# Retention and two feed-forward layers: attention by halves of 64 tokens, the first 512-token block through all of d_ff, operands of layer two kept as two halves

## The chip, the cores and the metric

One core of a Trainium2 chip runs the kernel. Its engines work side by side and meet at semaphores: PE (TensorE, matmuls), DVE (VectorE), ACT (ScalarE), POOL (GpSimd) and SP (SyncE, which only issues transfers). The metric is the device time of one execution in microseconds; the median of three runs counts.

## The reference, cut to what matters

Four batches of eight heads, 576 tokens each, head size 64: causal attention without softmax, in which a score decays with the distance. Its result, 2304 tokens of 512 numbers, goes through two feed-forward layers of width 2048. All in float32; the weights come as float64.

```python
scores = scale * np.matmul(q, k.transpose(0, 1, 3, 2))
gamma = 1.0 - 2.0 ** (-5.0 - np.arange(H, dtype=np.float32))
Dmat = np.where(rel >= 0, gamma[:, None, None] ** rel[None, :, :], 0.0)
attn_out = np.matmul(scores * Dmat, v)          # rel[i, j] = i - j
x = attn_out by tokens, heads side by side       # 2304 x 512
h = x @ w_in;  x = np.maximum(0.01 * h, h) @ w_out      # layer one
h = x @ w_in2; out = (h * np.cos(h)) @ w_out2           # layer two
```

## The kernel before

**Feed-forward.** The 2304 tokens lie in five blocks (`TB`, 384 or 512 tokens), d_ff in 16 tiles of 128 (`f`). A step of the program takes one block and one tile: `h_mm` (L327) forms h for it in 12 products, `o_mm` (L344) adds the tile of two steps before (three in layer two) to the block's output in 12 more, four banks of PSUM at a time. Twelve, since a float32 operand is split into a high half and a low rest, and three of the four combinations are formed for each of four pieces of 128: `split` (L232 on ACT, L233 on DVE) does it for x, `g_high` (L391, ACT) and `g_low` (L397, DVE) for g. In layer one g is 0.01 h on ACT (L381) and the larger of that and h on DVE (L382); in layer two the cosine by five DVE and three ACT instructions. `evacuate` copies a finished block out of PSUM and stores it.

**Attention** goes by chunks of 128 tokens and turns of two pairs of heads (`duo`), with a running state per pair. `scores` (L165) forms 128x128 scores and masks them on DVE (L170); `values` reads the state (L183), adds the values (L190, L191), forms the chunk's addition to the state (L196), scales the result on ACT (L205) and adds to the state on DVE (L215, L217). POOL scales q and v of a chunk ahead (L142, L146).

**Weights.** Each half tile (128x512 float64) is read as words (`load_raw`) and turned into float32 by two ACT instructions (`conv_a`: L255, L256) and four on DVE (`conv_b`: L261, L263, L266; `conv_c`: L273), then split by ACT (`conv_d`, L276) and, from the third on, POOL (`conv_e`, L280). Layer two's weights are converted the same way during layer one (`stash`), stored as float32, fetched again during layer one's last block and split there (`split_w`).

**Order.** Attention of the first block (three chunks) comes first, with products that nothing reads between its turns (`warm`, L226). Then six tiles of d_ff for block 0, all 16 for block 1, the other ten for block 0, whose two parts of output are added, and the other blocks; attention for the next block is spread over the steps. Up to step `MANUAL` = 22 the scheduler of the framework sets the order in each engine's queue, from then on that of the program. In either case an engine takes its queue strictly in order.

## Time and profile before

| | us |
|---|---|
| median of three runs | 924.25 (923.59 to 926.24) |
| span of the profiled execution | 923.9 |
| PE busy | 905.6 (98%) |
| DVE busy | 652.4 (71%) |
| ACT busy | 403.4 (44%) |
| POOL busy | 139.1 (15%) |

The profile is of one execution. A matmul's end in it is modelled, and consecutive matmuls overlap, so the pace of TensorE is better read from starts than from durations. The chain of work that ended last runs over PE for 87% of the span and over DVE for 10%.

### The profile page before, as it was taken

To read this page: it belongs to the slowest core of one execution; us is meant where nothing else is said; L and a number is where in the kernel's file an instruction comes from. 1 tells how busy PE (TensorE), PEld (TensorE's weight loads), DVE (VectorE), ACT (ScalarE), POOL (GpSimd) and SP (SyncE) were. 2 spreads that over 40 slices of the span, in tenths; PEclk is the share of its full clock that TensorE was granted. 3 is DMA by queue.
4 is the path that set the end of the run, shared out by engine and by line. 5 is a ranking of instruction groups with operands and counts; after the bars stand their busy time and mean duration, and the time that the engine had idled before them with its cause. 6 is when DMAs were issued, how large, how long until landed. Compare 5 with 4: busy or idle time off the path is not lost.

```text
span 923.9 us, 13238 instructions
## 1 busy us (share of the span) xinstructions
PE 905.6 (98%) x5052; PEld 772.6 (84%) x5052; DVE 652.4 (71%) x1155; ACT 403.4 (44%) x758; POOL 139.1 (15%) x112
## 2 busy tenths in 40 slices
PE   9899988999999999999999999999999999999998
PEld 8676866788987788999888888888889998888998
DVE  4988889556746566665222698788778889878885
ACT  3554655443433354444444643353334344334433
POOL 3555333112210011100144420000000000000000
PEclk9999999999999999999999999999999999999999
DMA  9356533146453445432333240020011001000100
GB/s 346 124 172 208 158 117 133 46 147 220 144 168 108 143 149 179 166 135 81 103 92 103 81 136 0 1 81 1 1 34 58 1 26 44 1 1 1 46 1 35
DMA packets 37951, 87.55 MB, mean 95 GB/s; under 512 B 4480, under 2 KB 9728, under 8 KB 37888
## 3 DMA queue, kind: packets, MB, share of 16 engines
q1 hardware_dynamic: 37312, 86.26, 27.7%
q8 instruction: 39, 0.64, 0.3%
q10 hardware_dynamic: 576, 0.45, 0.1%
q14 instruction: 24, 0.20, 0.1%
HBM read 67.30 MB, written 19.40 MB: 94 GB/s over the span
## 4 chain that ended last, share of the span: by engine, by line
PE 87%; DVE 10%; issue 2%; ACT 1%; DMA 0%; DVEq 0%; ACTq 0%
PE o L344 40%; PE h L327 28%; PE at L327 11%; DVE t L266 3%; PE at L165 2%; DVE t L273 2%; PE at L191 2%; DVE t L263 2%; DVE t L261 2%; PE at L183 2%; PE o L226 1%; PE at L196 1%; ACT t L255 1%; DVE x_sb L233 1%; DMA raw<-in_w 0%
## 5 line engine op out<-in xcount | busy, mean ns | idle before, releaser
L344 PE MATMUL o<-g,w 128*128 128x512 f32 (+1 forms) x1920 | 427.1, 370 | 5.0 <-DVE g L397 3.4
L344 PEld LDWEIGHTS o<-g,w 128*128 128x128 f32 x1920 | 348.7, 188 | 55.3 <-DVE g L397 7.1
L327 PE MATMUL h<-x_sb,w 128*128 128x512 f32 (+1 forms) x1440 | 323.6, 371 | 6.2 <-DVE x_sb L233 3.6
L327 PEld LDWEIGHTS h<-x_sb,w 128*128 128x128 f32 x1440 | 260.3, 188 | 47.3 <-DVE x_sb L233 5.1
L391 ACT CAST g<-graw 128x512 fp32r<-128x512 f32 (+1 forms) x160 | 92.5, 578 | 237.0 <-DVE graw L421 93.6
L397 DVE TENSOR_TENSOR g<-graw,g 128x512 fp32r<-128x512 f32 (+1 forms) x152 | 99.8, 657 | 40.3 <-ACT g L391 40.2
L280 POOL TENSOR_TENSOR w<-t,w 128x512 fp32r<-128x512 f32 x62 | 82.4, 1340 | 181.5 <-ACT w L276 175.8
L327 PE MATMUL at<-x_sb,w 128*128 128x512 f32 (+1 forms) x480 | 105.2, 367 | 0.0
L415 ACT ACTIVATE r_sb<-r_sb 128x512 f32<-128x512 f32 (+1 forms) x80 | 47.3, 591 | 131.8 <-DVE r_sb L414 131.8
L327 PEld LDWEIGHTS at<-x_sb,w 128*128 128x128 f32 x480 | 87.7, 188 | 11.5
L382 DVE TENSOR_TENSOR graw<-graw,h 128x512 f32<-128x512 f32 (+1 forms) x80 | 50.2, 627 | 43.5 <-ACT graw L381 43.5
L170 DVE TENSOR_TENSOR p_sb<-at,mask_sb 128x256 f32<-128x256 f32 x66 | 25.5, 418 | 60.7 <-PE at L165 60.6
L381 ACT ACTIVATE graw<-h 128x512 f32<-128x512 f32 (+1 forms) x80 | 44.2, 553 | 42.2 <-PE h L327 37.1
L266 DVE SCALAR_TENSOR_TENSOR t<-raw,t 128x512 uint32<-128x512 uint32 x64 | 57.9, 905 | 1.8
L255 ACT ACTIVATE t<-raw 128x512 f32<-128x512 f32 x64 | 42.9, 670 | 29.9 <-DMA raw<-in_w 27.5
L413 DVE SCALAR_TENSOR_TENSOR r_sb<-t_sb,r_sb 128x512 f32<-128x512 f32 (+1 forms) x80 | 52.1, 652 | 2.8
L414 DVE SCALAR_TENSOR_TENSOR r_sb<-t_sb,r_sb 128x512 f32<-128x512 f32 (+1 forms) x80 | 51.1, 639 | 2.7
L142 POOL TENSOR_TENSOR q_sb<-q_sb,itab_sb 128x512 f32<-128x512 f32 x18 | 25.9, 1441 | 169.3 <-DMA q_sb<-in_qt 165.5
L276 ACT CAST w<-t 128x512 fp32r<-128x512 f32 x64 | 39.0, 618 | 27.9 <-DVE t L273 26.8
L273 DVE CUSTOM_DVE_ANT_0 t<-raw,t 128x1024 uint16<-128x1024 uint16 x64 | 48.7, 762 | 2.4
L416 ACT ACTIVATE r_sb<-r_sb 128x512 f32<-128x512 f32 (+1 forms) x80 | 47.2, 589 | 2.5
L256 ACT ACTIVATE raw<-raw 128x512 int32<-128x512 uint32 x64 | 42.6, 666 | 1.8 <-DMA raw<-in_w 1.8
(52 smaller groups left out, 607.2 us busy)
## 6 DMA issues: line engine op xcount, KB each, us to landing
raw<-in_w SPq DMA_DIRECT2D x64, 512.0 KB, 3.4
kv_sb<-in_kv SPq DMA_DIRECT2D x16, 512.0 KB, 5.6
w<-t SPq DMA_DIRECT2D x32, 256.0 KB, 2.2
t<-w SPq DMA_DIRECT2D x32, 256.0 KB, 2.7
q_sb<-in_qt SPq DMA_DIRECT2D x18, 256.0 KB, 3.7
kt_sb<-in_kt SPq DMA_DIRECT2D x18, 256.0 KB, 4.1
x<-o_sb SPq DMA_DIRECT2D x12, 256.0 KB, 7.1
xr<-x SPq DMA_DIRECT2D x12, 256.0 KB, 4.5
```

The lines of the kernel that those rows point to most:

```text
L255: nc.scalar.activation(t, hi.bitcast(F32), AF.Abs)
L266: nc.vector.scalar_tensor_tensor(out=u, in0=words[:, :, 1], scalar=0xC0000000, in1=u, op0=ALU.bitwise_and, op1=ALU.bitwise_or)
L273: eng.tensor_tensor(out=i, in0=i, in1=lo, op=ALU.add)
L280: eng.tensor_tensor(out=wt[:, 1, s], in0=t_t.pop((l, f, s)), in1=wt[:, 0, s].bitcast(F32), op=ALU.subtract)
L327: nc.tensor.matmul(hp[:, :n], wt[:, i, 0, ks], x_t[lj, k][:, j, :n], start=(k == 0 and a == 0), stop=(k == KK - 1 and a == 2),)
L344: nc.tensor.matmul(o_t[lj, m][:, :n], wt[:, i, 1, ms], gt[:, j, :n], start=(f in starts and a == 0), stop=(f + 1 in ends and a == 2),)
L382: nc.vector.tensor_tensor(out=g, in0=g, in1=hp, op=ALU.max)
L391: nc.scalar.copy(g_t[lj, f][:, 0, : TB[lj % NB]], g)
L397: eng.tensor_tensor(out=gt[:, 1, :n], in0=graw.pop((lj, f)), in1=gt[:, 0, :n].bitcast(F32), op=ALU.subtract)
L413: nc.vector.scalar_tensor_tensor(out=r, in0=t, scalar=-C2, in1=r, op0=ALU.mult, op1=ALU.add)
L414: nc.vector.scalar_tensor_tensor(out=r, in0=t, scalar=-C3, in1=r, op0=ALU.mult, op1=ALU.add)
L415: nc.scalar.activation(r, r, AF.Sin, scale=0.5)
```

## The change

- **Attention by halves.** A chunk is still 128 tokens, but products are between halves of 64: scores only within a half, the state after each half (`state`, now four pairs wide, two additions of 128x256 a chunk instead of four of 128x64). Every product is 64x64x64 on a quarter of the array. All four head pairs go together; `scores`, `values` and the new `reads` are placed at three places of a step. q, k and v of a chunk come in one transfer of 1 MB.
- **Order.** Blocks are 512, 512, 512, 384, 384 tokens and each goes through all of d_ff at once, block 0 as well. The start does four chunks; the other 14 come at every third or fourth step. From step 0 on the order is that of the program.
- **Weights.** 15 of the 16 tiles of layer one are read and converted whole (1 MB, instructions of 128x1024), the last in two halves. The conversion keeps to four tiles in the start and then one a step; its last subtraction is on DVE.
- **Layer two's operands** are stored as the two halves that the products use: `stash_w` splits a converted half tile (ACT, POOL) and stores 512 KB, `fetch_w` reads them straight into place; `evacuate` of layer one splits x (ACT, DVE) and stores both halves, `load_x` reads both.
- **Prelu** on ACT replaces the product with 0.01 and the maximum. PSUM is one tile, its banks named by number. `G`, the buffers for what comes out of a product, is 4 instead of 5.

```diff
-TB = (384, 512, 512, 384, 512)
-T0 = (0, 384, 896, 1408, 1792)
+
+TB = (512, 512, 512, 384, 384)
+T0 = (0, 512, 1024, 1536, 1920)
...
-MANUAL = 22
...
-WARM = (28, 2, 6)
...
-G = 5
+WHOLE = NF - 1
...
+MANUAL = 0
...
+WARM = (16, 2)
...
+G = 4
...
+    psum = psp.tile([P, 8, 512], F32, name="psum")
...
+    def scores(i):
+        b, ch = banks_of(i), ch_t[i]
+        for p in range(NP):
+            for x in range(2):
+                for e, r in enumerate(halves):
+                    t = slice(p * P + x * C, p * P + (x + 1) * C)
+                    nc.tensor.matmul(
+                        psum[halves[x], b + e, p * C : (p + 1) * C],
+                        ch[r, 1, t],
+                        ch[r, 0, t],
+                        start=True,
+                        stop=True,
...
+            out=pt,
+            in0=psum[:, b : b + 2, : NP * C].rearrange("p e (n c) -> p e n c", n=NP),
+            in1=mask_sb.unsqueeze(1).unsqueeze(1).to_broadcast([P, 2, NP, C]),
+            op=ALU.mult,
...
+    def values(i):
+        b, ch, pt = banks_of(i), ch_t[i], p_t.pop(i)
+        local = [(2 * i + x) % SUBS for x in range(2)]
+        for p in range(NP):
+            for x, tok in enumerate(halves):
+                for e, r in enumerate(halves):
+                    h = slice((2 * p + e) * D, (2 * p + e + 1) * D)
+                    o = NP * C + p * C
+                    nc.tensor.matmul(
+                        psum[r, b + x, o : o + C],
+                        ch[tok, 3, h],
+                        pt[tok, e, p, :],
+                        start=p == 0,
+                        stop=local[x] == 0,
+                        skip_group_check=True,
...
+                        psum[r, b + x, p * D : (p + 1) * D],
+                        ch[tok, 2, h],
+                        ch[tok, 3, h],
...
+            new = ap.tile([P, NP * D], F32, tag="st", name="st", bufs=3)
+            add = psum[:, b + x, : NP * D]
+            if local[x] == 0:
+                summed[i] = nc.vector.tensor_copy(new, add)
+            else:
+                summed[i] = nc.vector.tensor_tensor(out=new, in0=add, in1=state[2 * i + x], op=ALU.add)
...
+    def reads(i):
...
+                    read = nc.tensor.matmul(
+                        psum[r, b + x, o : o + C],
+                        st[r, p * D : (p + 1) * D],
+                        ch[r, 0, t : t + C],
...
+    def load_raw(f):
+        if f < WHOLE:
...
+            raw = wp.tile([P, 2 * DM], I64, tag=f"w{tag}", name="raw")
+            nc.sync.dma_start(raw, w[0, f])
...
+    def stash_w(g):
+        t = t_t.pop(g)
+        both = rawp_t[g].rearrange("p (a n) -> p a n", a=2).bitcast(F32R)
+        nc.scalar.copy(both[:, 1], t)
+        nc.gpsimd.tensor_tensor(
+            out=both[:, 0], in0=t, in1=both[:, 1].bitcast(F32), op=ALU.subtract
+        )
+        nc.sync.dma_start(w2[g[1]][g[2]], rawp_t.pop(g).rearrange("p (a n) -> p a n", a=2))
+
+
+    def fetch_w(f):
+        new_w(1, f)
+        for s in range(2):
+            nc.sync.dma_start(w_t[1, f][:, :, s * DM : (s + 1) * DM].bitcast(F32), w2[f][s])
...
+            hi = gp.tile([P, n], F32R, tag="graw", name="x_hi", bufs=G)
...
+            nc.scalar.copy(hi, src)
+            nc.vector.tensor_tensor(out=lo, in0=src, in1=hi.bitcast(F32), op=ALU.subtract)
+            nc.sync.dma_start(x2[j][m][:, 0], hi.bitcast(F32))
+            nc.sync.dma_start(x2[j][m][:, 1], lo.bitcast(F32))
...
-        nc.scalar.mul(g, hp, 0.01)
-        nc.vector.tensor_tensor(out=g, in0=g, in1=hp, op=ALU.max)
+        nc.scalar.activation(g, hp, AF.Prelu, alpha=0.01)
...
+    grains = [(0, f, None) for f in range(WHOLE)]
+    grains += [(0, f, s) for f in range(WHOLE, NF) for s in range(2)]
...
-                    conv_e(*grains[k - 1], nc.vector if k < 3 else nc.gpsimd)
...
+                    conv_e(g, nc.vector)
...
-    turns = [(0, 0, PART), (1, 0, NF), (0, PART, NF)] + [(j, 0, NF) for j in range(2, NB)]
-    turns += [(NB + j, 0, NF) for j in (*range(1, NB), 0)]
...
+    turns = [*range(NB), *range(NB, 2 * NB)]
...
+            chunk_at[s1 + 2 + x * (NF - 4) // len(chunks[j + 1])] = i
...
+        warm(WARM[0], 3)
+        scores(0)
+        for i in range(n_first):
+            if i + 1 < n_first:
+                scores(i + 1)
+            warm(WARM[1], banks_of(i) ^ 4)
+            values(i)
+            conv(1)
+            warm(WARM[1], banks_of(i) ^ 4)
+            reads(i)
...
+                if s < NF:
+                    want = 2 * min(len(grains), max(n_first, s + 4)) + 1
+                    conv(min(1, want - halves_done[0]))
                 h_mm(lj, f)
...
+                leaky(lj, f)
+                if s < NF:
+                    conv(max(0, want - halves_done[0]))
+                g_high(lj, f)
+            for q in outs.get(s, ()):
+                o_mm(*q)
+            if i is not None:
+                reads(i)
+                if i + 2 < NCH:
+                    load_chunk(i + 2)
+                    ahead(i + 2)
+            if s + 1 in chunk_at:
+                scores(chunk_at[s + 1])
```

What it does to the rows of an engine is seen at three places.

PE in layer one, a place where attention stands between the groups of the feed-forward (`at` is the attention's bank, h and o the feed-forward's). Before, one turn of two head pairs:

```order
L165 MATMUL at<-q_sb,kt_sb 128x128 x4
L327 MATMUL h<-x_sb,w_774 128x384 x12
L183 MATMUL at<-q_sb,state_123 64x128 x2
L183 MATMUL at<-q_sb,state_124 64x128 x2
L191 MATMUL at<-p_sb,kv_sb 64x128 x4
L196 MATMUL at<-kv_sb 64x64 x4
L344 MATMUL o_1141<-g,w_1446 128x512 x3
```

Now (all banks are in `psum`; L160 are scores, L184 values, L198 the addition to the state, L227 reads of the state, L379 h and L393 o), one chunk:

```order
L160 MATMUL psum<-ch 64x64 x16
L379 MATMUL psum<-x_sb,w_679 128x512 x12
L184 MATMUL psum<-p_sb,ch 64x64 x16
L198 MATMUL psum<-ch 64x64 x16
L393 MATMUL psum<-g,w_567 128x512 x12
L227 MATMUL psum<-ch,st 64x64 x16
L379 MATMUL psum<-x_sb,w_744 128x512 x12
```

The reads of the state have moved behind the o group, the products are smaller and four times as many in a row.

DVE while layer one's weights are converted (t is a tile in conversion). Before, in block 1:

```order
L397 TENSOR_TENSOR g<-graw,g 128x512
L273 ISA t_1006<-raw,t_1006 128x1024
L382 TENSOR_TENSOR graw<-graw,h 128x512
L261 TENSOR_SCALAR t_1048<-t_1048 128x512
L263 TENSOR_SCALAR t_1048<-t_1048 128x512
L266 SCALAR_TENSOR_TENSOR t_1048<-raw,t_1048 128x512
L397 TENSOR_TENSOR g<-graw,g 128x512
L273 ISA t_1048<-raw,t_1048 128x1024
```

Now, in block 0, a step with a chunk (L300 to L312 convert, L324 is the last subtraction, L169 the mask, L214 the state, L439 the low half of g):

```order
L324 TENSOR_TENSOR w_785<-t_741,w_785 128x1024
L169 TENSOR_TENSOR p_sb<-psum,mask_sb 128x512
L300 TENSOR_SCALAR t_782<-t_782 128x1024
L302 TENSOR_SCALAR t_782<-t_782 128x1024
L305 SCALAR_TENSOR_TENSOR t_782<-raw,t_782 128x1024
L312 ISA t_782<-raw,t_782 128x2048
L214 TENSOR_TENSOR st<-psum,st 128x256 x2
L439 TENSOR_TENSOR g<-graw,g 128x512
L324 TENSOR_TENSOR w_880<-t_782,w_880 128x1024
```

The maximum is gone, the subtraction has come from POOL, the instructions are twice as wide, and the mask of the next chunk stands behind a whole conversion.

DVE at the end of the start, where x of the first block is split (L366). Now:

```order
L300 TENSOR_SCALAR t_514<-t_514 128x1024
L302 TENSOR_SCALAR t_514<-t_514 128x1024
L324 TENSOR_TENSOR w_517<-t_440,w_517 128x1024
L305 SCALAR_TENSOR_TENSOR t_514<-raw,t_514 128x1024
L366 TENSOR_TENSOR x_sb<-xr,x_sb 128x512
L312 ISA t_514<-raw,t_514 128x2048
L366 TENSOR_TENSOR x_sb<-xr,x_sb 128x512 x3
```

Before, the first block's x (L233) stood among the conversion of half tiles:

```order
L261 TENSOR_SCALAR t_420<-t_420 128x512
L233 TENSOR_TENSOR x_sb<-xr,x_sb 128x384
L263 TENSOR_SCALAR t_420<-t_420 128x512
L233 TENSOR_TENSOR x_sb<-xr,x_sb 128x384
L266 SCALAR_TENSOR_TENSOR t_420<-raw,t_420 128x512
L233 TENSOR_TENSOR x_sb<-xr,x_sb 128x384
```

Ahead of its last piece stand now four whole tiles in conversion, where there were five half tiles.

## Rows read from the trace of the kernel before

**Rows 1.** Stages: us, busy us (count) of PE, PEld, DVE, ACT, POOL; clock; DMA; GB/s.

```profile
31.20:86.60 55.40, 51.00 (x386) 37.92 (x385) 47.02 (x88) 28.57 (x64) 26.06 (x20) 0.97 0.47 158
86.60:184.50 97.90, 89.49 (x386) 70.80 (x385) 77.83 (x111) 54.17 (x98) 30.11 (x22) 1.00 0.36 124
184.50:911.50 727.00, 727.00 (x3961) 631.12 (x3961) 505.34 (x907) 302.20 (x560) 69.99 (x56) 1.00 0.24 78
911.50:923.90 12.40, 8.64 (x50) 8.19 (x48) 4.54 (x9) 4.31 (x9) 0.00 (x0) 0.99 0.18 64
```

**Rows 2.** PE in order of time, feed-forward alone; start, us, engine, line, operation.

```profile
448.77 2.88 PE L327 MATMUL h<-x_sb,w 128*128 128x512 f32 x12
...
454.21 2.88 PE L327 MATMUL h<-x_sb,w 128*128 128x512 f32 x12
...
715.88 2.24 PE L344 MATMUL o<-g,w 128*128 128x384 f32 x12
...
720.04 2.24 PE L344 MATMUL o<-g,w 128*128 128x384 f32 x12
```

**Rows 3.** PE in order of time, one turn of attention between two groups.

```profile
191.81 0.71 PE L165 MATMUL at<-q_sb,kt_sb 64*128 64x128 f32 x8
192.45 2.38 PE L327 MATMUL h<-x_sb,w 128*128 128x384 f32 x12
194.76 0.65 PE L183 MATMUL at<-q_sb,state 64*64 64x128 f32 x8
195.35 0.66 PE L191 MATMUL at<-p_sb,kv_sb 128*64 128x128 f32 x8
195.83 0.40 PE L196 MATMUL at<-kv_sb 128*64 128x64 f32 x8
196.16 3.02 PE L344 MATMUL o<-g,w 128*128 128x512 f32 x12
```

**Rows 4.** PE in order of time, values of a chunk that two sequences share.

```profile
53.07 0.27 PE L191 MATMUL at<-p_sb,kv_sb 128*64 128x64 f32 x1
53.08 0.27 PE L190 MATMUL at<-p_sb,kv_sb 128*64 128x64 f32 x1
...
53.24 0.22 PE L191 MATMUL at<-p_sb,kv_sb 128*64 128x64 f32 x1
...
53.30 0.27 PE L191 MATMUL at<-p_sb,kv_sb 128*64 128x64 f32 x2
```

**Rows 5.** DVE in order of time, block 1 during the conversion.

```profile
131.36 0.69 DVE L266 SCALAR_TENSOR_TENSOR t<-raw,t 128x512 uint32<-128x512 uint32 x1
131.97 0.69 DVE L397 TENSOR_TENSOR g<-graw,g 128x512 fp32r<-128x512 f32 x1
132.57 0.69 DVE L273 CUSTOM_DVE_ANT_0 t<-raw,t 128x1024 uint16<-128x1024 uint16 x1
133.17 0.68 DVE L382 TENSOR_TENSOR graw<-graw,h 128x512 f32<-128x512 f32 x1
133.77 0.42 DVE L261 TENSOR_SCALAR t<-t 128x512 f32<-128x512 f32 x1
134.22 1.40 DVE L263 TENSOR_SCALAR t<-t 128x512 uint32<-128x512 uint32 x1
```

**Rows 6.** ACT in order of time, the same place.

```profile
131.96 0.67 ACT L255 ACTIVATE t<-raw 128x512 f32<-128x512 f32 x1 [0.63 <-DMA raw<-in_w]
132.53 0.69 ACT L256 ACTIVATE raw<-raw 128x512 int32<-128x512 uint32 x1
133.29 0.62 ACT L276 CAST w<-t 128x512 fp32r<-128x512 f32 x1
```

**Rows 7.** POOL in order of time, the same place.

```profile
133.99 1.35 POOL L280 TENSOR_TENSOR w<-t,w 128x512 fp32r<-128x512 f32 x1 [3.41 <-ACT w L276]
```

**Rows 8.** Transfers at the start: a stretch, with GB/s last; raw tiles, median to landing.

```profile
5.00:10.00 5.00, 5.00 (x46) 4.88 (x46) 0.00 (x0) 0.00 (x0) 1.95 (x3) 1.00 0.99 355
...
raw<-in_w SPq DMA_DIRECT2D x6, 512.0 KB, 9.5
```

More of the change, by code (lines that the diff above doesn't have):

```diff
@@ new lines, in reads @@
+    def reads(i):
+        b, ch = banks_of(i), ch_t[i]
+        local = [(2 * i + x) % SUBS for x in range(2)]
+        for x in (1, 0):
+            if local[x] == 0:
+                continue
+            st = state.pop(2 * i + x)
+            for p in range(NP):
+                for r in halves:
+                    o, t = NP * C + p * C, p * P + x * C
+                    read = nc.tensor.matmul(
+                        psum[r, b + x, o : o + C],
+                        st[r, p * D : (p + 1) * D],
+                        ch[r, 0, t : t + C],
+                        start=False,
+                        stop=True,
+                        skip_group_check=True,
+                    )
+                    if i in summed:
+                        tc.add_manual_dep(
+                            read.ins, summed.pop(i).ins.name, IN_TURN, reason="other rows"
+                        )
@@ new lines, in retention_ffn_ffn @@
+    grains += [(0, f, s) for f in range(WHOLE, NF) for s in range(2)]
+    late = [(1, f, s) for f in range(NF) for s in range(2)]
+    ROOM = {}
+    for f in range(SPARE):
+        ROOM[f] = NF + 1 - n_first - f
+    for f in range(SPARE, WHOLE):
+        ROOM[f] = NF - 1 - (f - SPARE) % 2
+    halves_done, loaded, half_n = [0], [0], [0]
+    half_q = [g for g in grains if g[2] is not None] + late
+    def next_raw():
+        while loaded[0] < WHOLE:
+            f = loaded[0]
+            if f >= SPARE + 2 and (0, f - 2, None) in raw_t:
+                break
+            load_raw(f)
@@ L509, in retention_ffn_ffn @@
-    s0 = PART + NF - 1
-    joined = steps.index((2, 0, NF - 1)) + LAG[0]
-    free = [s for s in range(s0, last - 2) if not joined - 2 <= s <= joined]
+                    g = grains[k - 1]
+                    if not g[2]:
+                        new_w(0, g[1])
+                    conv_d(g)
+                    conv_e(g, nc.vector)
+            elif k < len(grains):
+                conv_b(grains[k])
+                conv_c(grains[k])
+                if grains[k][2] is None:
+                    next_raw()
+                else:
+                    next_half()
@@ new lines, in ahead @@
+    def ahead(i):
+        if n_first <= i < NCH:
+            scale_q(i)
+            scale_v(i)
+    turns = [*range(NB), *range(NB, 2 * NB)]
+    steps = [(lj, f) for lj in turns for f in range(NF)]
+    last = steps.index((NB - 1, 0))
+    chunks = [range(t0 // P, (t0 + n) // P) for t0, n in zip(T0, TB)]
+    chunk_at = {}
+    for j in range(NB - 1):
+        s1 = steps.index((j, 0))
+        for x, i in enumerate(chunks[j + 1]):
+            chunk_at[s1 + 2 + x * (NF - 4) // len(chunks[j + 1])] = i
@@ L512, in retention_ffn_ffn @@
+    outs = {}
+    for s, (lj, f) in enumerate(steps):
+        lag = LAG[lj // NB]
+        outs.setdefault(s + lag, []).append((lj, f))
+    s0 = NF + 1
+    free = [s for s in range(s0, last - 2)]
     stash_at = {}
@@ L606, in retention_ffn_ffn @@
             stash(s)
-            if s - 1 in outs and outs[s - 1][0] == NB - 1:
-                pf = outs[s - 1][1]
-                for k in range(2 * pf, 2 * pf + 2):
-                    split_w(*late[k][1:])
-                    if k + 2 < len(late):
-                        fetch_w(*late[k + 2][1:])
+            for qj, qf in outs.get(s - 1, ()):
+                if qj == NB - 1:
+                    fetch_w(qf)
 def kernel(**inputs):
```

503 lines of the change are left out of this document (196 added, 307 removed).

## The prediction

> **What bounds the kernel now.** I read the stages first [rows 1], then TensorE in order of time. From 184.5 us to 911.5 us TensorE is busy in every microsecond (727.00 of 727.00), though DVE works 505 us of that time; all of TensorE's idle time lies earlier: 4.4 us between 31.2 and 86.6 and 8.4 us between 86.6 and 184.5 (51.00 of 55.40, 89.49 of 97.90). So what counts is TensorE's own work, and, in the first 185 us, who keeps it waiting.
>
> Its main work has a fixed pace. A step is twelve products with w_in (an h group) and twelve with w_out (an o group): at 512 columns 5.44 us from one h group to the next (448.77 to 454.21), at 384 columns 4.16 from one o group to the next (715.88 to 720.04) [rows 2], so 2.72 and 2.08 a group. Before and after have the same blocks in another order: 96 steps of 512 and 64 of 384, 522.2 + 266.2 = **788.4 us**, which the change can't touch. Of the span of 923.9 us, 135.5 are left: 31.2 before the first product of the feed-forward, 3.8 behind the last (911.5 + 8.64 = 920.1 [rows 1]), and 100.5 of attention and waits in layer one.
>
> Attention is read from one turn of two head pairs [rows 3]. Scores: 0.64 us (191.81 to 192.45). The h group behind them takes 2.31 instead of 2.08, so 0.23 for the return to full tiles. State reads 0.59, values 0.48, state products 0.33 (194.76 to 196.16), and a second return, taken as 0.23 too. Sum 2.50 us a turn, 5.0 us for a chunk of 128 tokens. Fifteen chunks behind the first block's three make 75 us; 12.8 us are idle; the other 12.7 are groups that the scheduler cut into pieces before 184 us.
>
> **The change, part by part.** *Attention.* A chunk is now 64 products of 64x64x64. In the trace every such product is two matmuls. The question is how many run side by side. In [rows 4] a product into the lower half of a bank and one into the upper half begin 10 ns apart (53.07, 53.08), each half then goes on by itself, and a half's own matmuls follow every 0.05 to 0.06 us (one lasts 0.22, two in a row 0.27). So a tile of the array takes 55 ns a matmul and tiles don't wait for each other. Scores, values and state products now go round four such tiles, 8 matmuls each: 0.44 us apiece; the state reads go round two, 16 each: 0.88. Three excursions from the full tiles, where before there were four, cost 0.43 each: 0.20 that the scores take beyond their eight matmuls in two tiles (4 x 0.11, since 128 columns are twice 64) and the return of 0.23. A chunk: 2.20 + 1.29 = **3.5 us**. If only two of the four tiles run at once, 96 matmuls cost 2.64 instead of 1.32: 4.8 us. I take four, because [rows 4] show separate streams; the other end is a rival. Fourteen chunks now lie behind the first block's four: 14 x 3.5 = **49.0 us**.
>
> *The first block runs through all of d_ff.* Before, 32 half tiles of layer one's weights were converted in the start and over 22 steps, with most of the last subtractions on POOL; now 17 pieces, 15 of them of double width, must be done in the start and 14 steps, all on DVE. By [rows 5], taking double width as twice the row: 0.42 + 0.42 + 0.69 + 0.69 doubled is 4.44 us, the subtraction 1.38 (as L397), g's low half 0.69: 6.51 us a step. Chunks come every third step and bring a mask (0.69) and two state additions (0.4 each, from half of 0.69 and the fixed part): 1.5. Three steps: 21.0 us on DVE against 3 x 5.44 + 3.5 = 19.8 on TensorE. So here DVE is the bound. It also waits: the subtraction needs ACT's copy (0.62 doubled = 1.24 [rows 6]), which can't begin before the last integer step ends; 0.69 of that is covered by g's low half, 0.55 is not: three times, 1.65. That gives 22.7 us. On top, POOL's two scalings per chunk can hold DVE: the 0.4 us L263 took 1.40 while POOL's 1.35 us instruction ran [rows 5, 7]; at worst twice 0.98, 24.6 us. At best starts overlap (a 0.69 us row is followed 0.61 later [rows 5]), and 21.0 becomes 18.6, below TensorE. I take 22.7, nearest to rows that nothing disturbs: 2.9 us lost in each of 3.5 such rounds, **10 us**, with 0 and 17 as ends. TensorE itself has three tiles of weights in hand there; it feels a late DVE where values wait for the mask, which stands behind that step's conversion in DVE's row.
>
> *The start.* Before the last piece of x is split, DVE does four conversions (17.8), three subtractions (4.1), four masks, four x pieces (5.5) and seven state additions (2.8): 30.2 us, of which 29.5 stand behind the first raw tile. Raw 0 is third in the queue, behind 1 MB of chunk 0 and the table: 2.36 MB at 355 GB/s [rows 8] from 2 us on, so at 8.6; ACT needs 1.3 for its first half, and DVE begins at 9.9. 9.9 + 29.5 = 39.4; six scalings fall into it, and I charge half of them with 0.98: 42.4. The last x piece is wanted by the last 3 of 12 products, so the block runs as if it had begun at 40.4; 1.6 for hand-overs between the engines makes **42.0 us** (before: 31.2 with its first products drawn out). Ends: 38 with no lock and no hand-over, 46 with all six locks and raw 0 landing 9.5 us after its issue [rows 8].
>
> *Ends of blocks in layer one.* Instead of four ACT copies there are four copies, four DVE subtractions and eight stores, in four buffers instead of five; the fourth copy waits until the first store has landed. TensorE needs that bank again one h group and nine products later, about 5 us; a store that lands 2 us after its issue costs nothing, one of 8 us some 3. Four such ends at 1 us: **4 us** (0 to 12). Stores like these lie in the stages of [rows 1] where TensorE never waits.
>
> *Prelu, layer two's operands.* 80 DVE maxima (0.68 each) go; in the first block that is in the sum already. Layer two loses 20 copies and 20 subtractions for x and the split of 32 weight tiles in block four; they were under work that kept TensorE busy throughout [rows 1], so I cost them at nothing. The price is twice the bytes: 1 MB of weights per 4.16 us step of block four, 3.0 us at 355 GB/s; without that cover every step would lose what it is late. The order of layer two stays.
>
> **Sum:** 42.0 + 788.4 + 49.0 + 10 + 4 + 3.8 = 897.2 us, 26.7 below the span of 923.9. The median of the runs shown lies 0.35 above that span, so **897.6 us**.
>
> **Rivals.**
> *Two tiles at a time.* Row tiles 0 and 1 share the moving path or the queue can't feed four tiles, and halving the chunks gains nothing. For: no row shows more than two at once. Against: the independence in [rows 4]. Price: 1.32 us in each of the ten chunks behind the first block (there DVE hides it): 13 more, 910.8 us. The Trainium skill (TensorE: Matmul & The Clock Gate, Back-to-back issue gap) has a floor of about 25 ns between starts however few columns there are, which would give nearly this: 128 x 25 ns = 3.2 us, by its figure an estimate of 4.5 us a chunk. This trace doesn't show that floor between two tiles: 10 ns.
>
> *ACT and DVE take turns (slower than before).* In the first block ACT's first half of tile k+1 stands behind the Prelu of the step, and that behind the h group. If TensorE is late because DVE is late, ACT's part no longer runs beside DVE's, and a tile costs the whole chain: 2 x (0.67 + 0.69) = 2.7 on ACT, 4.44, 1.24, 1.38, and 0.69 for g: 10.5 us a step against 6.6 that TensorE needs. 13 steps lose 50 us instead of 10: 937.6 us. It ends above 924 once a step takes 9.4 us. For: raw tiles are asked for only when the tile two before is done, and in the first 30 us they took 9.5 us to land [rows 8], which pushes the same way. Against: raw tiles are asked for two tiles ahead, and in block one of before ACT and DVE did overlap (131.96 on ACT beside 131.97 on DVE [rows 5, 6]).
>
> *The conversion hides.* No lock, overlapping starts, a start at 38: 884 us.
>
> **How the numbers follow.** The forecast has 0.55, two tiles 0.20, taking turns 0.12, hidden 0.13. The range of 8 in 10 goes from the hidden case to past the two-tile case with a dear start: 884 to 919. A measurement of this kernel tells about 0.3% from no change, 2.8 us: faster (below 921.5) 0.84, the same 0.04, slower 0.12.
>
> **What would show it.** Right: scores rows of 32 matmuls within about 0.65 us up to the h group; three excursions, 3.5 us in all for a chunk; DVE over 90% busy from 12 to about 150 us; TensorE's idle time in the first block named after the mask or g's low half; no idle time from block one on but about 1 us at block ends; first h group ending near 45 us. Wrong: a chunk of 4.9 us; a step of the first block above 9 us; waits of the fourth copy for its store of over 3 us; waits for layer two's weights.

## The result, and the profile after

The changed kernel took 900.35 us, the median of four runs (897.84 to 903.23), against 923.92 for the kernel before in the same sessions: a ratio of 0.9733, 95% interval 0.9693 to 0.9772. Run again later, it took 898.21 (897.37 to 898.73), ratio 0.9718 (0.9705 to 0.9731). The forecast was 897.6 us, with 884 to 919 as its range.

The stages of the kernel after, in the columns of [rows 1]: two halves of the first block, a stretch of block one, and from 400 us on the last two blocks of layer one (one in part) and layer two, which begins at 493 us.

```profile
41.65:87.00 45.35, 41.89 (x368) 33.09 (x367) 39.68 (x41) 28.78 (x44) 9.64 (x6) 0.93 0.47 169
87.00:132.00 45.00, 40.17 (x403) 32.02 (x402) 39.57 (x43) 26.00 (x40) 9.10 (x6) 1.00 0.41 148
132.00:232.00 100.00, 99.86 (x863) 80.47 (x862) 46.31 (x73) 41.96 (x81) 18.30 (x14) 1.00 0.43 143
400.00:884.00 484.00, 483.29 (x2495) 436.83 (x2494) 340.47 (x601) 181.90 (x323) 5.43 (x4) 1.00 0.21 76
```

As before, TensorE is idle only near the front. From 132 us on it is busy nearly without a gap, though DVE is at half load or less in block one. In the first block DVE is busy for 79.25 of 90.35 us and TensorE stands idle for 3 to 5 us in each half; from 12 to 150 us DVE is busy for 116.57 of 138.00, 84%, where the prediction had over 90% as a sign of being right.

TensorE in order of time, the first groups of the first block and one of its rounds of three steps (L379 are h groups, L393 o groups, L160 scores, L184 values, L198 state products, L227 reads of the state):

```profile
38.53 8.63 PE L379 MATMUL psum<-x_sb,w 128*128 128x512 f32 x24 [3.52 <-DVE x_sb L366]
47.09 0.69 PE L160 MATMUL psum<-ch 64*64 64x64 f32 x32
47.71 3.02 PE L379 MATMUL psum<-x_sb,w 128*128 128x512 f32 x12
52.80 0.69 PE L184 MATMUL psum<-p_sb,ch 64*64 64x64 f32 x32 [2.06 <-DVE p_sb L169]
...
53.89 4.60 PE L393 MATMUL psum<-g,w 128*128 128x512 f32 x12
...
92.13 3.02 PE L379 MATMUL psum<-x_sb,w 128*128 128x512 f32 x12
97.07 0.69 PE L184 MATMUL psum<-p_sb,ch 64*64 64x64 f32 x32 [1.93 <-DVE p_sb L169]
97.56 0.68 PE L198 MATMUL psum<-ch 64*64 64x64 f32 x32
98.16 3.06 PE L393 MATMUL psum<-g,w 128*128 128x512 f32 x12
101.69 1.15 PE L227 MATMUL psum<-ch,st 64*64 64x64 f32 x32 [0.47 <-DVE st L214]
...
114.49 3.02 PE L379 MATMUL psum<-x_sb,w 128*128 128x512 f32 x12
```

The first named wait is the one that the prediction looked for, the mask (L169). The other is for the state addition (L214); the prediction had named g's low half in its place. The same view in block one, where nothing waits, answers to [rows 3]:

```profile
158.01 0.69 PE L160 MATMUL psum<-ch 64*64 64x64 f32 x32
158.64 3.02 PE L379 MATMUL psum<-x_sb,w 128*128 128x512 f32 x12
161.59 0.69 PE L184 MATMUL psum<-p_sb,ch 64*64 64x64 f32 x32
162.10 0.63 PE L198 MATMUL psum<-ch 64*64 64x64 f32 x16
162.67 3.02 PE L393 MATMUL psum<-g,w 128*128 128x512 f32 x12
165.62 1.15 PE L227 MATMUL psum<-ch,st 64*64 64x64 f32 x32
166.69 3.02 PE L379 MATMUL psum<-x_sb,w 128*128 128x512 f32 x12
...
178.43 3.02 PE L379 MATMUL psum<-x_sb,w 128*128 128x512 f32 x12
```

Three steps with a chunk take 178.43 - 158.64 = 19.79 us; less 3 x 5.44, the chunk costs 3.47.

Term by term, read from this execution (span 896.1):

| term | forecast, us | measured, us | read from |
|---|---|---|---|
| first block, as if begun at | 42.0 | 41.65 | 24 products end at 47.09, less 24 x 0.227 |
| products of the feed-forward | 788.4 | 788.4 | a step: 5.44 us from 141.60 to 147.04, 4.17 from 439.03 to 443.20 |
| stalls of the first block | 10 | 10.4 | 41.65 to 130.72, less 24 groups and four chunks |
| fourteen chunks | 49.0 | 50.5 | what is left |
| ends of blocks | 4 | 1.6 | two waits for x_lo, 1.2 and 0.4 |
| behind the last product | 3.8 | 3.6 | 892.54 to 896.1 |
| span | 897.2 | 896.1 | |

(The first chunk begins a sequence and reads one state instead of two, 0.46 us less: the four are 13.4 us.)

### The profile page after: what moved, and what is told of

The parts are those of the page before. It is cut to its first block, busy times and chain, and to the rows that moved or that the text cites. A ratio compares the mean times of both kernels' runs of the same rounds, so it can differ in the third digit from the quotient of the medians.

```text
span 896.1 us, 14836 instructions
## 1 busy us (share of the span) xinstructions
PE 868.2 (97%) x6080; PEld 756.4 (84%) x6080; DVE 590.6 (66%) x944; ACT 387.0 (43%) x689; POOL 98.4 (11%) x72
## 4 chain that ended last, share of the span: by engine, by line
PE 82%; DVE 8%; DMA 4%; ACT 3%; issue 1%; POOL 1%; SPq 0%; ACTq 0%; DVEq 0%; POOLq 0%
PE psum L393 39%; PE psum L379 39%; DMA ch<-in_qkv 2%; PE psum L227 2%; DMA raw<-in_w 1%; DVE t L312 1%; DVE w L324 1%; DVE t L305 1%; DMA x<-x_hi 1%; ACT w L321 1%; DVE t L302 1%; DVE t L300 1%; DVE st L214 1%; PE psum L184 1%; ACT raw L295 1%
## 5 line engine op out<-in xcount | busy, mean ns | idle before, releaser
L379 PE MATMUL psum<-x_sb,w 128*128 128x512 f32 (+1 forms) x1920 | 426.7, 371 | 3.6 <-DVE x_sb L366 3.5
L393 PE MATMUL psum<-g,w 128*128 128x512 f32 (+1 forms) x1920 | 424.2, 369 | 1.9 <-DVE x_lo L418 1.6
L379 PEld LDWEIGHTS psum<-x_sb,w 128*128 128x128 f32 x1920 | 350.1, 189 | 50.9 <-DVE x_sb L366 4.5
L393 PEld LDWEIGHTS psum<-g,w 128*128 128x128 f32 x1920 | 350.2, 188 | 48.8 <-DVE x_lo L418 2.2
L439 DVE TENSOR_TENSOR g<-graw,g 128x512 fp32r<-128x512 f32 (+1 forms) x160 | 109.4, 684 | 97.7 <-ACT g L434 97.5
L447 DVE TENSOR_SCALAR t_sb<-psum 128x512 f32<-128x512 f32 (+1 forms) x80 | 51.0, 637 | 63.0 <-PE psum L379 63.0
L425 ACT ACTIVATE graw<-psum 128x512 f32<-128x512 f32 (+1 forms) x80 | 44.1, 552 | 58.6 <-PE psum L379 56.6
L336 POOL TENSOR_TENSOR t<-t 128x512 fp32r<-128x512 f32 x32 | 45.3, 1420 | 113.3 <-ACT t L335 82.7
L300 DVE TENSOR_SCALAR t<-t 128x512 f32<-128x512 f32 (+1 forms) x49 | 35.1, 717 | 29.7 <-ACT t L294 29.6
L454 DVE SCALAR_TENSOR_TENSOR r_sb<-t_sb,psum 128x512 f32<-128x512 f32 (+1 forms) x80 | 50.8, 635 | 2.7
L135 POOL TENSOR_TENSOR ch<-ch,itab_sb 128x512 f32<-128x512 f32 x18 | 28.4, 1579 | 207.8 <-DMA ch<-in_qkv 202.2
L463 DVE SCALAR_TENSOR_TENSOR graw<-r_sb,psum 128x512 f32<-128x512 f32 (+1 forms) x80 | 50.0, 625 | 1.7 <-ACT r_sb L458 1.7
L312 DVE CUSTOM_DVE_ANT_0 t<-raw,t 128x1024 uint16<-128x1024 uint16 (+1 forms) x49 | 44.7, 912 | 4.7
L169 DVE TENSOR_TENSOR p_sb<-psum,mask_sb 128x512 f32<-128x512 f32 x18 | 12.4, 689 | 51.9 <-PE psum L160 41.4
L305 DVE SCALAR_TENSOR_TENSOR t<-raw,t 128x512 uint32<-128x512 uint32 (+1 forms) x49 | 43.4, 885 | 1.6
```

What stands on the lines that cost most here:

```text
L305: nc.vector.scalar_tensor_tensor(out=u, in0=hi, scalar=0xC0000000, in1=u, op0=ALU.bitwise_and, op1=ALU.bitwise_or)
L312: nc.vector.tensor_tensor(out=i, in0=i, in1=lo.bitcast(I32), op=ALU.add)
L379: nc.tensor.matmul(hp, wt[:, i ^ hi, ks], x_t[lj, k][:, j, :n], start=(k == 0 and a == 0), stop=(k == KK - 1 and a == 2),)
L393: nc.tensor.matmul(psum[:, BANK_O + m, :n], wt[:, i ^ hi, ms], gt[:, j, :n], start=(f == 0 and a == 0), stop=(f == NF - 1 and a == 2),)
L439: nc.vector.tensor_tensor(out=gt[:, 1, :n], in0=graw.pop((lj, f)), in1=gt[:, 0, :n].bitcast(F32), op=ALU.subtract)
L447: nc.vector.tensor_scalar(t, h_t[lj, f], INV_2PI, MAGIC, op0=ALU.mult, op1=ALU.add)
```

## The experiments

All are edits of the changed kernel. Where the first block ends is told by the start of block one's first h group in the profiled run, 147.0 us in the profile above. Medians:

| kernel | us | runs | block one from, us |
|---|---|---|---|
| same_again | 898.2 | 897.4 to 898.7 | 146.3 |
| scores_early | 895.2 | 893.3 to 895.9 | 144.3 |
| pool_sub | 902.1 | 901.5 to 902.9 | 151.3 |
| warm_gap | 898.3 | 897.5 to 902.5 | 145.0 |
| tile_by_tile | 923.4 | 919.7 to 926.3 | 151.0 |
| early_later | 890.3 | 889.9 to 891.3 | 141.0 |
| ahead3 | 894.3 | 893.1 to 897.4 | 144.8 |
| no_prelu | 917.7 | 915.3 to 919.6 | 150.6 |
| early_apart | 901.6 | 900.3 to 902.6 | 145.6 |
| together | 891.8 | 891.0 to 892.8 | 139.4 |
| three_first | 891.2 | 890.8 to 891.5 | 139.6 |
| load_first | 889.1 | 887.5 to 890.7 | 139.8 |

**The changed kernel again.**

> The changed kernel once more, to have its spread beside the others. Theory: the runs between 897.8 and 903.2 us differ in the granted clock of the start, so the spans should again go with the clock (0.990 at 896, 0.986 at 901). Rival: they differ in the transfers of layer one's weights; then spans of 4 us difference show at equal clocks. Either way a median of 898 to 902 us.

898.2 us, as expected, and the four runs lie within 1.4 us, so the spread of the first four (897.8 to 903.2) has not come back, and this run can't tell the two theories apart. Two spans at nearly the same clock (896.6 and 900.2 us at 0.989) speak against the first. The runs below are compared with this one. Only scores_early, pool_sub and warm_gap were timed in the same session; in the four sessions the kernel before took 924.2, 924.6, 924.7 and 924.3 us, so differences of half a microsecond between sessions mean nothing.

**Do four quarters of the array work side by side?**

```diff
-        for p in range(NP):
-            for x in range(2):
-                for e, r in enumerate(halves):
+        for x in range(2):
+            for e, r in enumerate(halves):
+                for p in range(NP):
```

(in scores, values and state products)

> Scores, values and state products of a chunk in another order: all eight matmuls of one quarter of the array, then those of the next, instead of going round the four. Theory of the forecast (a quarter takes 55 ns a matmul and four work side by side, as long as neighbours in the queue are for different quarters): 32 matmuls one behind the other take 1.76 us instead of 0.44 to 0.5, a chunk 3.5 + 3.9 = 7.4 us, ten chunks behind the first block 39 us more, about 937 to 950 us. Rival (matmuls leave one queue every 14 to 20 ns whatever quarter they are for, the next quarter's begin while the last one's still run): the three groups keep 0.5 to 0.6 us and the time stays at 897 to 901.

The same products in another order cost 25 us. TensorE in order of time, a chunk of this kernel:

```profile
227.50 1.54 PE L160 MATMUL psum<-ch 64*64 64x64 f32 x32
228.97 3.06 PE L379 MATMUL psum<-x_sb,w 128*128 128x512 f32 x12
231.96 1.36 PE L184 MATMUL psum<-p_sb,ch 64*64 64x64 f32 x29
233.11 0.27 PE L198 MATMUL psum<-ch 64*64 64x64 f32 x1
233.16 0.22 PE L184 MATMUL psum<-p_sb,ch 64*64 64x64 f32 x1
...
233.22 0.22 PE L184 MATMUL psum<-p_sb,ch 64*64 64x64 f32 x1
...
234.57 3.01 PE L393 MATMUL psum<-g,w 128*128 128x512 f32 x12
```

Scores take 1.47 us up to the h group instead of 0.63, values and state products 2.61 instead of 1.09: 2.36 more a chunk (1.8 in three chunks that have half as many state products). The span grew by 22.8. The ten chunks behind the first block make 22.0 of dearer products, of which 3.2 take the place of waits that the changed kernel run again had there. The start's chunks go tile by tile as well, and its first two h groups end 4.7 us later (50.69 against 46.00); from there to block one both kernels take 100.28 us, so in the first block DVE's lateness hides the dearer products. That makes 23.5; 0.7 too much is not placed. So the rival falls: matmuls for one quarter follow each other every 0.055 us (233.16, 233.22; the pace of [rows 4]), and only neighbours for other quarters run beside them. The 3.9 us of the expectation were too many. In these rows state products for the next quarter begin at 233.11, while the last three values still wait for theirs. If that holds at each change of quarter, three matmuls are let past each time: 8 + 3 x 5 slots of 0.055 and the 0.20 of the excursion give 1.47 for the scores, 8 + 7 x 5 slots give 2.57 for the other two, where 2.61 was measured.

**What does an excursion from the full tiles cost?** early_apart differs from early_later (below) only in that the state products stand alone:

```diff
                 if i is not None:
                     values(i)
-                    sums(i)
...
             for q in outs.get(s, ()):
                 o_mm(*q)
+            if i is not None:
+                sums(i)
```

> Beside early_later: the state products no longer follow the values but stand alone behind the o group, so that each of the 14 chunks leaves the full tiles four times instead of three; the same matmuls otherwise. Theory of the forecast (0.43 us for each time that TensorE goes to quarters of the array and back): 14 x 0.43 = 6.0 us more than early_later's 890.3, 895 to 897. Rival (only the return costs, 0.23, or the products fill a gap): 890 to 894.

11.3 us more, twice what was expected. By rows a fourth excursion costs 0.39 us: three steps with a chunk take 20.19 us (211.16 to 231.35) against 19.80 in early_later (205.31 to 225.11). Fourteen of them are 5.5 us. The rest are waits, since the state is ready one o group later (9.1 us from the first mask on, 5.5 in early_later), and the clock: behind the longest wait, 2.65 us at 80.52, the granted clock was 0.50 until 82.42 and 0.80 until 86.00, and the reads and the o group there took 1.5 us more than usual. The first block ends 4.7 us later, of which four excursions are 1.6. The two profiled runs differ by 10.0 us, the medians, from two sessions, by 11.3. So 0.43 was near, and the total was not a measure of it.

**Why does TensorE wait in the first block?** The chain of work that ended last in the changed kernel, followed through one round (start, us, what; "issue" is time without a visible cause):

```profile
101.69 1.15 PE psum L227 x32
102.84 2.96 PE psum L379 x12
...
106.31 1.16 ACT t L294
107.47 1.02 ACT raw L295
108.50 0.94 ACT w L321
...
109.46 1.23 DVE w L324
110.69 1.71 DVE t L300
...
112.42 1.43 DVE t L302
...
116.39 1.06 ACT w L321
...
117.48 1.22 DVE w L324
118.70 0.61 DVE p_sb L169
...
119.45 0.69 PE psum L184 x32
```

It goes from TensorE to ACT, to DVE, to ACT and to DVE again before the mask lets TensorE on. That is not DVE at work without a pause. Three experiments move what TensorE waits for.

```diff
                 h_mm(lj, f)
+                if s + 1 in chunk_at:
+                    scores(chunk_at[s + 1])
...
-            if s + 1 in chunk_at:
-                scores(chunk_at[s + 1])
```

> Scores of a chunk, and with them the mask on DVE, are issued one group of TensorE earlier (between the h group and the o group of the step before), so the mask stands ahead of a tile's last subtraction and of the next tile's conversion. Theory of the forecast (DVE's work bounds the first block): the 6.9 us that values wait for the mask come back as waits for the state or for g's low half; the first h group of block one still begins at 145 to 147 us, the time falls by 0 to 2 us. Rival (DVE has room, the mask merely stood behind the wrong work): that group begins at 140 to 142 us and the time falls by 5 to 7 us.

3.0 us less, between the two. No wait for the mask is left; those for the state are 10.7 us in the whole run, 6.3 in the changed kernel run again. The state addition is wanted one o group after its products and stands behind a conversion as well. So the reads were moved too, and with them the transfer and POOL's scaling of the chunk after next, which stand behind them in the program (early_later: scores_early, and)

```diff
                 h_mm(lj, f)
+                if s - 1 in chunk_at:
+                    reads(chunk_at[s - 1])
...
-            if i is not None:
-                reads(i)
```

> Scores one group earlier, and besides the reads of the state one h group later (behind the next step's h group), so that neither the mask nor the state additions on DVE are wanted at once. Theory of the forecast (DVE's work bounds the first block; a round of three steps takes it 21 to 22 us against 19.8): TensorE loses the same elsewhere, 5 to 7 us of stalls stay, block one's first h group begins at 142 to 144 us, 893 to 895 us. Rival (DVE's lateness of some us never reaches the weights, which are three tiles ahead; only the place of mask and additions lets TensorE feel it): stalls of 0 to 2 us, that group at 136 to 139 us, 887 to 890 us.

7.9 us less than the changed kernel, and block one begins 5.3 us earlier: nearer to the rival, place, though not all of it. From the first mask on TensorE waits 4.0 us in the first block instead of 8.7, and no group there is slowed by the clock, which costs 1.6 us in the changed kernel run again (more on this below). The moved transfer and scaling were not tried apart. The rounds still take 20.77 and 21.56 us (67.24 to 88.01 to 109.57) against 19.80 without waits.

```diff
-                    want = 2 * min(len(grains), max(n_first, s + 4)) + 1
+                    want = 2 * min(len(grains), max(n_first, s + 3)) + 1
```

> One number: from the first step on, the conversion keeps one tile less in hand, so every mask and state addition has one conversion less (5.8 us of DVE) ahead of it in DVE's row. Theory of the forecast (DVE's work bounds the first block): DVE stands idle once for up to 5 us and the same work ends later, the time moves by 0 to +4 us. Rival (place): the waits for the mask of the first two rounds go (3 us) and the later ones shrink, 892 to 895 us.

4.0 us less by the medians, 2.5 between the profiled runs, and 1.5 of it in the first block: DVE has less ahead of the first mask, which then isn't waited for (51.20, right behind the h group of 48.26), and later rounds are as before. Place again, once.

**Would POOL or a quicker TensorE help?**

```diff
-                    conv_e(g, nc.vector)
+                    conv_e(g, nc.vector if k <= n_first else nc.gpsimd)
```

> The last subtraction of the conversion goes to POOL from the fifth tile on (12 pieces). Theory of the forecast (DVE's work bounds the first block): DVE has 3.7 us less in each round of three steps, 22.4 becomes 18.7 to 19.8, the stalls of 9.9 us fall to 2 to 4, the time falls by 6 to 8 us. Rival (POOL holds DVE while it works, as L300 took 1.78 us instead of 0.69 beside POOL's L135): three subtractions of 2.7 us a round hold DVE by about 1 us each, and TensorE waits for late tiles: the time moves by -1 to +4 us.

3.9 us more: the rival's number. POOL and DVE of this kernel in order of time:

```profile
96.53 2.88 POOL L324 TENSOR_TENSOR w<-t,w 128x1024 fp32r<-128x1024 f32 x1 [3.61 <-ACT w L321]
```

```profile
95.89 0.68 DVE L169 TENSOR_TENSOR p_sb<-psum,mask_sb 128x512 f32<-128x512 f32 x1
96.49 0.68 DVE L300 TENSOR_SCALAR t<-t 128x1024 f32<-128x1024 f32 x1
97.21 2.75 DVE L302 TENSOR_SCALAR t<-t 128x1024 uint32<-128x1024 uint32 x1
```

L302 takes 2.75 us instead of 0.69: POOL's subtraction ends at 99.41, and L302 0.55 later, as if it had begun only then. The 1.23 us that DVE was spared came back as 2.06. So DVE is no earlier, but TensorE does not wait longer either: from the first mask on, its waits in the first block come to 8.7 us here and to 8.7 in the changed kernel run again. They all stand before the reads of the state now, none before the values, and what grew is the time behind them:

```profile
126.73 1.15 PE L227 MATMUL psum<-ch,st 64*64 64x64 f32 x32 [1.81 <-DVE st L214]
127.81 4.61 PE L379 MATMUL psum<-x_sb,w 128*128 128x512 f32 x12
```

An h group behind reads takes 2.86 us up to the next row when it is undisturbed (125.14 to 128.00 in the changed kernel), here 4.45 (to 132.26), and the mean granted clock from 126.73 to 132.30 was 0.69. The same came behind the other three waits (0.59, 0.68, 0.62). Together these groups are 6.2 us slower than at full clock; in the changed kernel run again it is 1.6, behind the first wait alone. That difference of some 4.7 us is nearly all of the 5.0 by which block one begins later.

```diff
         split_x(0)
+        warm(20, 6)
```

> Twenty more products on zeros between the last state reads of the start and the first h group, where TensorE stands idle for 3.5 us; nothing else. Theory A (the granted clock of 0.58 behind that gap costs 3.1 us in the first two h groups and 1.8 in the first o group, and the path runs over them): 3 to 5 us less, the first o group 2.7 instead of 4.5 us, and spans that lie closer together. Theory B (DVE bounds the first block, so TensorE only arrives earlier at the same waits): the first h groups are as quick, but the wait for the first mask grows by as much, and the time falls by 0 to 1 us.

No difference (898.3 against 898.2), as theory B had it. The granted clock in the changed kernel (stages, columns of [rows 1]) does show the loss:

```profile
38.50:41.00 2.50, 2.38 (x5) 1.47 (x6) 2.50 (x4) 2.50 (x3) 0.00 (x0) 0.50 1.00 419
...
45.00:47.10 2.10, 2.10 (x12) 1.47 (x10) 2.07 (x2) 0.69 (x2) 2.10 (x2) 1.00 0.93 347
...
54.00:56.00 2.00, 2.00 (x6) 1.63 (x7) 1.95 (x2) 0.31 (x1) 0.00 (x0) 0.62 0.01 4
```

Behind 3.5 us without products it is at 0.50, the lower of its two levels, and at 1.00 again after some 6 us of work. Behind the wait for the first mask it is at 0.62, partly at the lower level, and the o group at 53.89 takes 4.53 us up to the next row, where 2.94 is usual (52.30 to 55.24 in ahead3). In warm_gap the clock stays at 1.00 in both places. The first 24 products end at 45.38, 1.7 us earlier than in the profile above (47.09) and 0.6 earlier than in the changed kernel run again (46.00), but the next scores then wait 1.4 us for POOL's scaling (L135), and values still wait for the mask. Block one begins 1.3 us earlier than in the run again, and 1.0 us more of waits behind the first block take most of that back. A faster TensorE arrived earlier at the same queue. Its runs reach from 897.5 to 902.5 all the same, so the clock in that gap doesn't explain either why runs of the changed kernel differ by 5 us; that stays open.

**Prelu undone.**

```diff
-        nc.scalar.activation(g, hp, AF.Prelu, alpha=0.01)
+        nc.scalar.mul(g, hp, 0.01)
+        nc.vector.tensor_tensor(out=g, in0=g, in1=hp, op=ALU.max)
```

> Prelu undone: 0.01 h on ACT and the maximum on DVE, as in the kernel before; the rest as changed. Theory of the forecast (DVE's work bounds the first block): 14 steps by 0.68 us are 9.5 us more on DVE, the time rises by 7 to 10 us. Rival (place): only the one or two maxima of a round that stand between the conversion and the next mask or addition are felt, 3 to 5 us more. Outside the first block neither expects a difference.

19.5 us more, past both. In the first block it is 4.3, near the rival's 3 to 5. The rest lies behind it, where neither theory saw any: waits of 13.4 us in six places up to 400 us (3.2 in the changed kernel run again), and the clock. Behind the four longest of these waits the granted clock was 0.52 to 0.71, and the groups there took 6.8 us more than the same groups at 1.00. What led to the longest, on ACT and on DVE (the idle time before an instruction and what ended it stand last):

```profile
186.62 0.66 ACT L294 ACTIVATE t<-raw 128x512 f32<-128x512 f32 x1 [7.87 <-DMA raw<-in_w]
```

```profile
188.34 0.69 DVE L426 TENSOR_TENSOR graw<-graw,psum 128x512 f32<-128x512 f32 x1 [8.79 <-ACT graw L425]
188.94 0.68 DVE L169 TENSOR_TENSOR p_sb<-psum,mask_sb 128x512 f32<-128x512 f32 x1
```

ACT stands before a raw half tile of layer two's weights that hasn't landed. The product with 0.01 is queued behind that on ACT, the maximum behind the product stops DVE, and the next mask stands behind the maximum: TensorE waits 4.8 us at 189.77. With Prelu only ACT stands still, DVE goes on to the mask, and the o group that wants g comes two steps later.

**Put together.** together is early_later, ahead3 and warm_gap at once; three_first is together with one tile fewer in the start, at both places where the start converts, and the steps' count lowered by one to match:

```diff
-            conv(1)
+            if i < 3:
+                conv(1)
```

> early_later, one tile less in hand, and the twenty products on zeros in the gap before the first h group, all three. Theory that the runs so far speak for (place: TensorE feels DVE's lateness only through what stands close ahead of it in DVE's row, and the slow clock of the first groups counts once they are not followed by waits): the remaining waits of 4 us for the state fall below 1.5, the first groups lose 3 us less, 884 to 887. Rival (DVE's work bounds the first block, rounds of 21 us against 19.8): what is won at the front is lost before block one, 888 to 891.

> together, and only three tiles converted before the first h group instead of four; the fourth follows in the steps. Theory of place: x of the first block is split 4 to 6 us earlier, DVE has the same work left over one step more and stays within the tiles in hand, 880 to 883. Rival (DVE's work now is the bound: some 90 us of it behind the start against 84 us of TensorE's steps): h groups wait for weights, or the waits for mask and state come back, 884 to 889.

Here the theory of place fails: 891.8 and 891.2, a little above the ranges of both rivals (888 to 891, 884 to 889) and no better than early_later's 890.3. Block one begins 1.5 us earlier, so the front gained little, and the rounds are still 20.75 and 21.14 us (together, 66.00 to 86.75 to 107.89). What is left with the mask and the additions moved is put down to DVE's pace with its pauses; no run tests that by itself. three_first is not a clean test: DVE was done with the last piece of x at 39.98, 1.4 us earlier than in the changed kernel and not 4 to 6, since two instructions of the fourth tile (36.16 to 37.57) still stand ahead of x.

together also lost 2.0 us at the end of a block, where TensorE waited for x_lo on DVE, and 1.4 more in the two groups behind that wait. The raw half tiles come late because SP's queue stands before stores: 177.8 us between 150 and 400 in the changed kernel. load_first is together with 12 products on zeros and

```diff
             conv_c(g)
+            next_half()
             stash_w(g)
-            next_half()
```

> together with fewer products on zeros in the gap (12 instead of 20), and in layer one's later blocks SP asks for the next raw half tile before the store of the last one, which waits for POOL. Theory (ACT, and behind it DVE, stand still because raw half tiles are asked for late: SP stood 178 us in front of those stores): the raw tiles come some 5 us earlier, the waits of TensorE behind block zero for the subtraction of x_lo and for the state (2.4 and about 1 us in together) go, 886 to 889 us. Rival (the late tiles are not what holds DVE at the ends of blocks, its own queue is): 890 to 892 as together.

889.1, against 891.8. SP's queue before and now (changed kernel, then load_first; waits between 150 and 400 us: total, times, longest):

```profile
SPq L339 <- POOL t L336: 177.8, 28, 12.8
```

```profile
SPq L343 <- POOL t L340: 105.8, 29, 11.1
SPq L285 <- DVE t L316: 62.2, 22, 6.2
```

In together, from which load_first differs, the stores cost 174.8 us. So SP stands still at these places for nearly as long as before (168.0), but 62.2 of it now in front of loads (L285), which wait for DVE to be done with their buffer and no longer for a store. ACT waited 38.1 us for raw half tiles there in the changed kernel and 18.8 in together; in load_first no such wait is left, only 7.4 us for stores that hold its buffers. Of TensorE's waits for x_lo one of 0.4 us is left. This is the lowest median of these kernels, 0.962 of the kernel before (0.9606 to 0.9633); early_later has 0.9616 (0.9592 to 0.964) and runs that overlap, so which of the two is faster is not shown. Fewer products on zeros and the moved load were not timed apart.

## Why the prediction was right, point by point

**Attention.** Right in mechanism and size: 3.47 us a chunk against 3.5. The two-tile rival (4.8) falls by the rows of block one and by tile_by_tile. The floor of about 25 ns between starts (the Trainium skill, TensorE: Matmul & The Clock Gate, Back-to-back issue gap) doesn't hold between quarters: 32 scores and the entry are over in 0.63 us, and 32 x 25 ns would be 0.80. Three excursions at 0.43 were nearly right; a fourth measured 0.39. The fourteen chunks came to 50.5 instead of 49.0: 48.1 by 3.47 a chunk, 1.0 of small waits for the state behind the first block, 0.3 of one wait for g's low half; 1.1 is not placed.

**The start.** 41.65 against 42.0, by two errors that met. DVE was done with the last piece of x at 41.42, not 42.4, as double-width instructions cost less than twice. But 1.6 us were charged for hand-overs, and what stood there was mostly TensorE's clock at half speed, of which the sum knew nothing: 1.7 us between this profile and warm_gap, 0.6 in the changed kernel run again.

**The first block's stalls.** 10.4 against 10, and here the step was wrong though the number was right; that they met is luck. The 10.4 are 6.9 of waits for the mask, 1.4 of waits for the state, 1.6 of the lower clock behind the first mask wait, for which the sum had no term, and 0.5 not placed; g's low half, which the prediction named too, let TensorE wait nowhere there. The sum made DVE's work the bound: 21.0 us a round, 1.65 of waits for ACT's copy, nothing for POOL. DVE of the changed kernel in order of time, the end of the round that the chain above goes through:

```profile
109.46 1.23 DVE L324 TENSOR_TENSOR w<-t,w 128x1024 fp32r<-128x1024 f32 x1 [1.65 <-ACT w L321]
110.60 1.78 DVE L300 TENSOR_SCALAR t<-t 128x1024 f32<-128x1024 f32 x1
112.42 1.41 DVE L302 TENSOR_SCALAR t<-t 128x1024 uint32<-128x1024 uint32 x1
```

Undisturbed, L300 and L302 take 0.69 each. The round has 18.8 us of work by durations (5.74 a step, 1.62 for mask and additions), 18.4 by starts, as instructions overlap: less than TensorE's 19.8. To this come 2.2 of waits for ACT (0.51 and the 1.65 here) and 1.8 of POOL's hold (1.09 and 0.72 here). DVE did come to 22.4, but through pauses. Where TensorE felt it, "values wait for the mask", was foreseen; that moving the mask and the reads would let block one begin 5.3 us earlier was not. The widths were off as well: of [rows 5], 0.42 us at 512 columns became 0.69 at 1024 and 0.69 became 1.23, where twice the row was taken.

**ACT and DVE take turns.** The rival's time (937.6) was far off, but the chain above shows its mechanism at a low price: ACT's copy of a tile stands behind its first half of the next, DVE's subtraction behind that copy. To put the copy first on ACT was not tried.

**Ends of blocks.** 1.6 instead of 4. The fourth copy did wait for the first store, up to 3.5 us, which the prediction named as a sign against itself; it cost TensorE one wait of 1.2 us.

**Edits costed at nothing.** Layer two: right, TensorE was busy for 483.29 of the 484.00 us from 400 on, and in layer two one wait of 0.3 us is left. Prelu: the maxima were taken for 0.68 us each in the first block and for nothing behind it. Within the changed kernel they are worth 19.5 us, 4.3 of them in the first block: a maximum ties DVE's queue to ACT's, and the clock falls behind the waits. This price stayed out of the result only because the change takes the maxima out.

**From the span to the median.** Taken as 0.35, it was 4.25 in the first four runs and 1.9 in the later ones. This is the whole miss of 2.75 us: the span itself came out 1.1 below the sum. Each of the first four executions took 1.7 to 2.0 us longer than its own span (897.84 against 896.1 for the profiled one), and executions of the kernel before about 2.1 (924.23 against 922.1). The 0.35 set a median beside the span of another execution, and the profile after is of the fastest of its four runs, which makes the other 2.5.

## What to carry to other kernels

Small products on quarters of the array pay only if neighbours in the queue go to different quarters. A sum of an engine's work can give the right wait for the wrong reason; look in its row at what stands ahead of the instruction that others want, and move that first. An operation that joins two engines' queues costs, besides its own time, every wait of the first engine that the second then shares. And a wait of TensorE can cost more than its length: in pool_sub the waits of the first block were no longer in sum than in the changed kernel run again, and the block took 5.0 us more, since the granted clock fell behind four of them instead of one. Why it fell behind the waits of 1.81 and 1.85 us there and not behind those of 1.81 and 1.91 in the other run is open.

## What was not expected of the hardware

- An engine was said to take its queue strictly in order. Matmuls of different quarters don't start in the order of the program: in tile_by_tile a state product begins at 233.11, and values that were issued before it at 233.16, 233.22 and once more.
- POOL's hold on DVE lasts for the whole of POOL's instruction. In pool_sub L300 (2.86 us instead of 0.69), L302 (2.75 instead of 0.69) and L305 (3.30 instead of 1.23) each end about their own length after POOL's, while the L300 that began at 96.49, just before POOL's at 96.53, took its usual 0.68. The Trainium skill (SBUF — State Buffer, Who interferes with whom) has a port pair that the first of the two holds for its whole instruction, while the other stands still; the trace agrees with these numbers. The forecast's 0.98 for one hold, from a shorter POOL instruction, was of that kind but too small for POOL at double width.
- DVE's instructions gain from width: with one operand 0.42 us for 512 columns and 0.69 for 1024, with two 0.69 and 1.23, some 0.15 less than twice in both.
